# The first loads and steps of a fused attention and rational-MLP kernel, put in another order on one Trainium2 core

## The chip, the cores and the metric

The kernel runs on one NeuronCore of a Trainium2 chip. The metric is the device time of one execution in microseconds. The kernel before was timed three times: 251.33, 251.53 and 252.5, median 251.53.

## The reference

```python
def phi(x):
    a = np.einsum('rd,bhsd->bhsr', S1, x)
    b = np.einsum('rd,bhsd->bhsr', S2, x)
    return np.einsum('bhsi,bhsj->bhsij', a, b).reshape(*x.shape[:-1], r * r)
q_p, k_p = phi(q), phi(k)
kv = np.einsum('bhsf,bhsd->bhfd', k_p, v)
z = np.sum(k_p, axis=2)
attn = (q_p @ kv) / (q_p . z + 1e-6)
x = attn, heads side by side: (4352, 128)

h = x @ w_in
P = a[0] + a[1] * h + a[2] * h**2 + a[3] * h**3
Q = 1.0 + abs(b[0]) * abs(h) + abs(b[1]) * h**2
out = (P / (Q + 1e-06)) @ w_out
```

q, k and v are (4, 4, 1088, 32) in float32: 4 batches, 4 heads, 1088 tokens of 32 values. S1 and S2 are 8 x 32. w_in is 128 x 2048, w_out 2048 x 128. So there is a linear attention with quadratic sketch features, and behind it a two-layer network with a rational activation.

## The kernel before

**Stages.** Each batch goes through key steps, query steps and then the network. Key steps (class `Keys`): `kt` transposes a part of k in 32 x 32 blocks on DVE (L315), `ks` multiplies it with S1 and S2 on PE (L323), `kc` copies half of that from PSUM on ACT (L330), `kf` multiplies the halves on DVE to the features k_p (L335), and `kp` multiplies k_p with v on PE, the key products (L364). `kk` copies the result to kvz on ACT (L374). The first batch has k in four transposes and three parts, so that the work can begin before all of k is there: parts 0 and 1 hold two column blocks each, part 2 the other five.

**Queries.** Tokens go in blocks; the first batch has four. For each: `qt` transpose (DVE, L387), `qs` sketches (PE, L400), `qc` copy (ACT, L407 or L410), `qf` features (DVE, L416 or L419), `qp` products with kvz (PE, L428), `qd` the denominator plus 1e-6, `qi` its reciprocal, `qx` the quotient (DVE, L444, L449), `qb` transpose back (PE, L455) and `qk` copy to xT (ACT, L462). The fourth block and all later batches use class `Spread`, whose sketches (L473) go through DRAM (sk_d) and come back as `a_all` and `b_all` (L484 to L490).

**The network.** For each unit of up to 512 tokens, `h` multiplies xT with w_in on PE (L519), `e` casts the result to bf16 on ACT (L525), and DVE and ACT form the rational function (`u`, `ln`, `ex`, `rd`, `s`, `pd`, `m`, `v`, `x`); `G` multiplies with w_out on PE (L677) and `st` stores. `wo` scales the halves of w_out by constants that are computed from a and b.

**Order.** The program is written out by hand: the string `ORDER` lists all steps, each with an index, and every engine gets its instructions in that order. An engine works its list in order, so an instruction that waits holds up all behind it on that engine. Loads are steps too: `lk`, `lv`, `lq`, `lx` (w_in), `lw` (w_out); they are issued by SP. Eight semaphores serve all loads of SP and ACT in turn, so a load can have to wait until an earlier one with the same semaphore has landed.

**The first loads** stand ahead of `ORDER` (L196 to L214). SP issues S2, three quarters of k (240 KB, L201), 512 columns of the first q (256 KB, L206) and the four loads of v (L187). ACT issues S1, the first columns of each k block (256 KB, L199), the rest of k (48 KB, L203), a, b, and then loads its function table (L213). One load of v brings one column block m for all heads to 32 partitions; source and destination both begin with a dimension of 32:

```python
for m in range(NM):
    w = min(W, (NJ - m * NT) * D)
    nc.sync.dma_start(out=t[m * 32:(m + 1) * 32, :, 0:w], in_=vv[:, :, m * W:m * W + w])
```

**Idle products.** `tn` multiplies a tile of zeros on PE, 128 x 512 in bf16 (L225); `TURNS` says how many: 11 for `tn:0` and 2 for `tn:4`, all at the very start.

**Constants.** `ba` takes the absolute value of b on ACT (L818) and then runs a row of tiny steps on GpSimd (L759 to L772); `bi` takes a reciprocal on DVE (L775) and ends them. A second variant of the whole program (`General`) follows under a condition and isn't executed for these inputs.

Of the kernel before, what the change touches and what calls it, by code (L numbers as in the profile page):

```python
# [28 lines left out]
pd0:0 u0:0 kc0:1 kc1:1 kf0:1 m0:0 kt0:2 ln1:0 h0:1 e2:1 kt1:2 ex1:0 e0:1 v0:0 rd1:0 h1:1 ks1:2 qs:4 kf1:1 h3:1 qt:5  # L29
e1:1 h1:2 v1:0 u0:1 qf:3 qc:4 ln0:0 kc1:2 e3:1 ex0:0 kp1:1 qp:3 pd1:1 kf1:2 h3:2 ln0:1 s1:0 e1:2 rd0:0 qd:3 qi:3 G3:0  # L30
h0:2 ex0:1 e3:2 kk:1 e0:2 G0:0 x1:0 G5:0 qx:3 u1:1 qf:4 qs:5 qp:4 s0:0 u0:2 ln1:1 h2:2 lq:2 lk:3 qc:5 qd:4 qi:4 ex1:1
qt:7 qx:4 qb:3 qk:3 qb:4 lv:2 qk:4 x0:0 rd0:1 m1:1 ks0:2 qs:7 e2:2 u1:2 ln0:2 rd1:1 h2:3 v0:1 h0:3 e2:3 h1:3 v1:1
kc0:2 kf0:2 kt1:3 s1:1 ex0:2 qt:9 qf:5 e0:3 e1:3 kt0:3 ln1:2 G3:1 G2:0 h3:3 x1:1 h0:4 qc:7 e3:3 h3:4 ra0:2 st:0 qp:5
ex1:2 qd:5 qi:5 e0:4 ra1:2 kp1:2 s0:2 qx:5 G0:2 qs:6 u1:3 pd1:2 e3:4 qb:5 h1:4 qk:5 m0:2 G0:1 m1:2 h0:5 s1:2 qf:7
ln0:3 qc:6 e1:4 ln1:3 h2:4 x0:2 v1:2 G2:1 e0:5 ex1:3 qt:8 x1:2 pd1:3 h3:5 G1:2 kk:2 e2:4 ks0:3 ex0:3 qp:7 u1:4 e3:5
qs:8 ln0:4 rd0:3 rd1:3 h2:5 qd:7 e2:5 G3:2 qf:6 qc:8 s1:3 h1:5 G2:2 kc0:3 ln1:4 G5:1 kf0:3 qi:7 e1:5 lq:3 ex0:4 ex1:4
h1:6 G5:2 m1:3 h3:6 qx:7 u1:5 G3:3 ra0:4 qs:9 qp:6 x1:3 G0:3 rd1:4 G2:3 e1:6 ln0:5 st:2 pd1:4 lv:3 s1:4 h0:6 e3:6
ln1:5 qd:6 qi:6 qb:7 qf:8 G4:3 qx:6 qk:7 h2:6 m1:4 e0:6 qc:9 G0:4 ex1:5 qb:6 qk:6 qp:8 qt:10 ks1:3 h2:7 e2:6 G3:4
ex0:5 u1:6 x1:4 e2:7 h0:7 qd:8 ln1:6 G5:3 rd1:5 qi:8 h3:7 G1:4 G5:4 qt:12 G1:3 e0:7 G2:4 pd1:5 rd0:5 ex1:6 e3:7 h1:7
m1:5 kc1:3 ra1:6 qf:9 ln0:6 qx:8 e1:7 qp:9 qs:10 ex0:6 v0:5 qd:9 h1:8 s1:5 G4:4 u1:7 pd1:6 qc:10 h3:8 e1:8 st:4 qt:11  # L40
v1:5 rd0:6 qi:9 qb:8 G3:5 ln0:7 kf1:3 e3:8 ln1:7 h0:8 h2:8 x1:5 qk:8 qs:11 e0:8 ex1:7 kp1:3 s1:6 qx:9 G0:5 e2:8 G5:5
ex0:7 h2:9 kk:3 qf:10 h3:9 u1:8 qb:9 ra0:7 m0:6 G0:6 ra1:7 qs:12 m1:6 qc:11 x0:6 ln0:8 v1:6 e3:9 pd1:7 e2:9 qp:10 qk:9
qd:10 s1:7 G2:5 ln1:8 x1:6 G3:6 h0:9 qi:10 e0:9 h1:9 m1:7 ex0:8 qx:10 e1:9 pd1:8 v1:7 h1:10 u1:9 e1:10 rd0:8 ex1:8
rd1:8 G0:7 h0:10 G2:6 ln1:9 G3:7 e0:10 G1:6 ex1:9 qb:10 v0:7 h2:10 qk:10 e2:10 h3:10 s1:8 G5:6 qf:11 qp:11 ln0:9 h3:11
rd1:9 e3:10 h0:11 qd:11 ex0:9 m1:8 qi:11 e3:11 e0:11 u1:10 G3:8 G4:8 h2:11 x1:7 h1:11 x0:7 G2:7 ln1:10 qc:12 rd0:9
ln0:10 x1:8 e2:11 e1:11 G0:8 s1:9 ex1:10 ex0:10 G5:7 G1:8 h1:12 qx:11 qb:11 ra1:10 pd1:9 h0:12 qk:11 m1:9 u1:11 G0:9
x1:9 e1:12 G2:8 e0:12 h3:12 h2:12 rd0:10 qf:12 ln1:11 ln0:11 G5:9 G5:8 G1:9 s1:10 e2:12 G3:9 qp:12 ex0:11 pd1:10 e3:12
G0:10 ex1:11 m1:10 u1:12 rd0:11 h2:13 G3:10 ln1:12 ln0:12 e2:13 h3:13 qd:12 e3:13 G4:9 G2:9 rd1:11 h1:13 ex0:12 x1:10
h0:13 st:6 e1:13 s1:11 u1:13 ex1:12 pd1:11 m1:11 e0:13 G3:11 rd0:12 h2:14 ln1:13 h3:14 e2:14 G2:10 u0:13 ln0:13 G4:10
e3:14 qi:12 G1:11 x1:11 G1:10 rd1:12 qx:12 h1:14 ex1:13 st:8 s1:12 pd1:12 ex0:13 h0:14 e1:14 G0:11 qb:12 e0:14 ra0:13  # L50
rd1:13 G1:12 G5:10 G5:11 G4:11 qk:12 G3:12 h0:15 u1:14 ln0:14 m1:12 ln1:14 st:10 h1:15 x1:12 G0:12 G2:11 e0:15 h3:15
G4:12 ex1:14 e1:15 h2:15 s1:13 ex0:14 G3:13 pd1:13 m0:13 u0:15 G5:12 rd1:14 m1:13 e3:15 ln0:15 h1:16 e2:15 G4:13 G0:13
# [18 lines left out]
class General:  # L71
    FAST = False
    TURNS = (11, 0, 0, 0, 2, 0, 0, 0, 0)
# [49 lines left out]
def run(  # L123
# [26 lines left out]
    NM = 4  # L150
# [43 lines left out]
    for i, s_in in enumerate((S1, S2)):  # L194
        t = consts.tile([128, D], FP, name=f"s_raw{i}")
        (nc.scalar, nc.sync)[i].dma_start(out=t, in_=bass.AP(tensor=s_in.tensor, offset=s_in.offset,  # L196
                                                             ap=[[0, 16], [D, R], [1, D]]))
        s_raw.append(t)
# [75 lines left out]
    b_fit, c_fit, c_inv = (consts.tile([128, 2], FP, name=x) for x in ("b_fit", "c_fit", "c_inv"))  # L274
    a_k = consts.tile([128, 3], FP, name="a_k")
    special = consts.tile([128, 1], mybir.dt.int32, name="special")
    k_in_reg, k_sq_reg = (nc.scalar.alloc_register(x) if fast else None for x in ("k_in_reg", "k_sq_reg"))
    a1, a2, a3 = a_sb[:, 1:2], a_sb[:, 2:3], a_sb[:, 3:4]
# [299 lines left out]

    def on_act(i, h):
        return plan.P_ON_ACT[2 * i + (h > 0)]  # L580
# [68 lines left out]
    @skip()  # L649
    def d_v(i, h, hh):  # L650
        if horner(i, h):
            g = part_of(i, "g", h)
            nc.vector.tensor_scalar(out=g, in0=g, scalar1=a1, scalar2=None, op0=AX.add)

    @skip(plan.WIDE_X, horner)
    def d_g(i, h, hh):
        g = part_of(i, "g", h)
        nc.vector.tensor_mul(out=g, in0=g, in1=part_of(i, "s" if horner(i, first(h)) else "p", h))  # L658

    def terms(i):  # L660
# [96 lines left out]
    def fitting():  # L757
        g = nc.gpsimd
        g.tensor_mul(out=sq, in0=ab0, in1=ab0)  # L759
# [5 lines left out]
        by(fit, b4, AX.is_ge, sq, AX.mult, fit)  # L765
        by(lim, fit, AX.mult, -1.0, AX.add, 1.0)
# [3 lines left out]
        g.tensor_copy(out=special, in_=lim)  # L770
        by(c_fit[:, 1:2], b4, AX.mult, 1.0 + 1e-6, AX.subtract, sq)
        g.tensor_copy(out=c_fit[:, 0:1], in_=b_fit[:, 0:1])  # L772

    def factors():
# [3 lines left out]
        nc.gpsimd.tensor_copy(out=a_k[:, 2:3], in_=k_out)  # L778
        by(k_in, b4, AX.mult, 0.5, AX.mult, c_inv[:, 0:1])
        by(k_sq, sq, AX.mult, c_inv[:, 1:2])  # L780

    def registers():
        nc.scalar.reg_load(k_in_reg, k_in[0:1, :].bitcast(mybir.dt.int32))
        nc.scalar.reg_load(k_sq_reg, k_sq[0:1, :].bitcast(mybir.dt.int32))
        if any(plan.P_ON_ACT):
            nc.scalar.reg_load(a3_reg, a_sb[0:1, 3:4].bitcast(mybir.dt.int32))
# [9 lines left out]
    does = {"e": evac, "h": hidden, "u": d_abs, "w": d_w, "y": d_y, "ln": a_square if fast else a_ln, "ex": a_root if fast else a_exp, "ra": a_inv, "rd": d_inv, "pa": a_p, "pd": d_p,  # L796
# [7 lines left out]
    for step in plan.ORDER:  # L804
# [63 lines left out]
```

## Time and profile before

| | |
|---|---|
| median of three runs | 251.53 us |
| the profiled execution | 251.9 us, of which its span 250.0 |
| busy PE, DVE, ACT, GpSimd | 240.5, 233.0, 227.9, 7.5 us |
| first product of the network (L519) | starts at 18.05 us in the chain |
| moved by DMA | 19.60 MB |

All times inside the kernel count from the start of the span. In a list of work the columns are start, duration, engine, line, operation, tiles, count, and in brackets the idle time of the engine in front of it with what ended that time. PE is the matmul array, PEld its weight load, which runs beside it, SPq and ACTq are the DMA issues of SP and ACT. A float32 product appears as two passes, so 36 instructions give 72 entries. In the chain of waits each piece is the one that the next had to wait for.

### The profile page before, as it was taken

How to read it: one execution, taken by the hardware profiler on the slowest of the kernel's cores; microseconds unless marked ns; L12 is line 12 of the kernel's file. 1: busy time of each engine (PE TensorE's matmuls, PEld its weight loads, DVE VectorE, ACT ScalarE, POOL GpSimd, SP SyncE). 2: the span in 40 equal slices, each digit the busy share in tenths (PEclk: the TensorE clock that was granted, in tenths of full speed). 3: DMA queues.
4: the chain of work that ended last, by engine and by line, in shares of the span. 5: the costliest groups of instructions: out<-in, count | busy, mean ns of one | idle time of the engine just before them, and what ended most of it. 6: DMA issues, size and time to landing. Idle time of an engine off the chain costs nothing.

```text
span 250.0 us, 4083 instructions
## 1 busy us (share of the span) xinstructions
PE 240.5 (96%) x1585; PEld 133.8 (54%) x1585; DVE 233.0 (93%) x233; ACT 227.9 (91%) x217; POOL 7.5 (3%) x43
## 2 busy tenths in 40 slices
PE   7889999999999999999999999999999999999990
PEld 2668546645645455445555344444544467666770
DVE  3776999899999999999999999999999999999990
ACT  2267999999999999999999999999999999999980
POOL 4340000000000000000000000000000000000000
PEclk9999999999999999999999999999999999999999
DMA  5995348464413176210512200030020211020032
GB/s 155 257 387 89 99 121 188 134 156 78 144 27 100 28 202 138 69 45 16 148 22 77 67 3 0 16 102 3 0 42 0 40 25 22 0 37 8 0 49 42
DMA packets 30534, 19.60 MB, mean 78 GB/s; under 512 B 20400, under 2 KB 26672, under 8 KB 30512
## 3 DMA queue, kind: packets, MB, share of 16 engines
q1 hardware_dynamic: 28864, 18.92, 30.4%
q10 hardware_dynamic: 1648, 0.40, 0.9%
q8 instruction: 13, 0.21, 0.4%
q14 instruction: 9, 0.07, 0.1%
HBM read 16.16 MB, written 3.15 MB: 77 GB/s over the span
## 4 chain that ended last, share of the span: by engine, by line
PE 77%; DVE 13%; DMA 3%; issue 3%; SPq 0%; DVEq 0%
PE h_ps L519 42%; PE att_ps L677 23%; PE att_ps L428 4%; DVE g L658 4%; PE att_ps L364 4%; DVE g L647 3%; DVE s L643 2%; DMA k_sb<-in_k_dram 2%; PE att_ps L455 2%; DMA v_sb<-in_v_dram 2%; PE att_ps L473 2%; PE att_ps L323 1%; DVE p L600 1%; DVE r L630 1%; DVE out_sb L686 1%
## 5 line engine op out<-in xcount | busy, mean ns | idle before, releaser
L519 PE MATMUL h_ps<-xT,w_in_sb 128*128 128x512 f32 (+1 forms) x320 | 125.8, 532 | 0.0
L519 PEld LDWEIGHTS h_ps<-xT,w_in_sb 128*128 128x128 f32 x320 | 59.3, 190 | 44.4 <-issue 34.0
L525 ACT CAST hh<-h_ps 128x1024 bf16<-128x1024 f32 x68 | 72.2, 1086 | 2.1 <-PE h_ps L519 1.9
L613 ACT ACTIVATE ln<-u 128x2048 f32<-128x2048 bf16 (+1 forms) x35 | 67.2, 1950 | 0.0
L677 PEld LDWEIGHTS <-w_out 128*128 128x128 bf16 x432 | 41.8, 98 | 46.0 <-issue 16.5
L618 ACT ACTIVATE r<-ln 128x2048 bf16<-128x2048 f32 x22 | 44.0, 2002 | 0.0
L643 DVE TENSOR_TENSOR s<-hh,r 128x4096 bf16<-128x4096 bf16 (+2 forms) x21 | 39.2, 1872 | 0.0
L677 PE MATMUL att_ps<-r,w_out 128*128 128x512 bf16 (+1 forms) x160 | 34.8, 347 | 0.1
L677 PE MATMUL att_ps<-g,w_out 128*128 128x512 bf16 (+1 forms) x160 | 34.4, 347 | 0.0
L647 DVE TENSOR_TENSOR g<-hh,s 128x4096 bf16<-128x4096 bf16 (+2 forms) x16 | 27.8, 1744 | 0.3 <-PE att_ps L677 0.3
L658 DVE TENSOR_TENSOR g<-g,p 128x4096 bf16<-128x4096 bf16 (+2 forms) x15 | 27.7, 1849 | 0.0
L630 DVE TENSOR_TENSOR r<-r 128x2048 bf16<-128x2048 bf16 x22 | 26.5, 1217 | 0.0
L677 PE MATMUL att_ps<-s,w_out 128*128 128x512 bf16 (+1 forms) x112 | 24.5, 349 | 0.4 <-DVE s L643 0.4
L618 ACT ACTIVATE ln<-ln 128x2048 f32<-128x2048 f32 (+1 forms) x13 | 24.4, 1895 | 0.0
L624 ACT ACTIVATE r<-ln 128x2048 bf16<-128x2048 f32 (+1 forms) x13 | 23.7, 1868 | 0.0
L600 DVE TENSOR_SCALAR p<-hh,a_sb 128x4096 bf16<-128x4096 bf16 (+1 forms) x17 | 21.6, 1273 | 0.6 <-ACT hh L525 0.6
L548 DVE TENSOR_SCALAR u<-hh 128x2048 uint16<-128x2048 uint16 (+2 forms) x24 | 21.7, 905 | 0.4 <-ACT hh L525 0.4
L647 DVE TENSOR_TENSOR g<-hh,p 128x2048 bf16<-128x2048 bf16 (+1 forms) x7 | 11.6, 1663 | 0.0
L658 DVE TENSOR_TENSOR g<-g,s 128x2048 bf16<-128x2048 bf16 (+1 forms) x8 | 11.6, 1463 | 0.0
L428 PEld LDWEIGHTS att_ps<-kvz,q_pT 128*64 128x64 f32 x288 | 9.8, 137 | 3.3 <-issue 1.7
L428 PE MATMUL att_ps<-kvz,q_pT 128*64 128x66 f32 x288 | 11.1, 224 | 0.0
L364 PE MATMUL att_ps<-v_sb,k_p 128*64 128x64 f32 (+1 forms) x288 | 9.2, 222 | 1.0 <-DMA v_sb<-in_v_dram 1.0
(79 smaller groups left out, 146.6 us busy)
## 6 DMA issues: line engine op xcount, KB each, us to landing
a_all<-sk_d SPq DMA_DIRECT2D x6, 384.0 KB
b_all<-sk_d SPq DMA_DIRECT2D x12, 192.0 KB
v_sb<-in_v_dram SPq DMA_DIRECT2D x12, 144.0 KB
k_sb<-in_k_dram SPq DMA_DIRECT2D x3, 544.0 KB
q_sb<-in_q_dram SPq DMA_DIRECT2D x3, 544.0 KB
a_all<-sk_d SPq DMA_DIRECT2D x4, 320.0 KB
b_all<-sk_d SPq DMA_DIRECT2D x8, 160.0 KB
w_out_sb_f<-in_moe_w_out_dram SPq DMA_DIRECT2D x2, 512.0 KB
```

The costliest lines, as they stand in the source:

```text
L428: nc.tensor.matmul(self.nd[g * 64:(g + 1) * 64, o:o + 2 * KW], lhsT=self.q_p[:, c, x + g * 64:x + (g + 1) * 64], rhs=kvz[self.b % 2][:, c, ...
L519: nc.tensor.matmul(t[:, x * tl:(x + 1) * tl], lhsT=w_in_sb[:, f * 128:(f + 1) * 128], rhs=xT[:, x_at(t0):x_at(t0) + tl], start=True, stop= ...
L525: nc.scalar.copy(out=live[i]["hh"][:, part * PW:(part + 1) * PW], in_=live[i]["h", part])
L600: nc.vector.tensor_scalar(out=part_of(i, "p", h), in0=hh, scalar1=a3, scalar2=a2, op0=AX.mult, op1=AX.add)
L613: nc.scalar.activation(out=t, in_=live[i]["u"][:, span(h)], func=ACT.Square, scale=k_in_reg, bias=1.0)
L618: nc.scalar.activation(out=t if r_on_act(i, h) else part_of(i, "r", h), in_=t, func=ACT.Abs_reciprocal_sqrt, scale=k_sq_reg, bias=1.0)
L624: nc.scalar.activation(out=part_of(i, "r", h), in_=live[i]["ln", h], func=ACT.Square)
L630: nc.vector.tensor_mul(out=t, in0=t, in1=t)
L643: nc.vector.tensor_mul(out=part_of(i, "s", h), in0=hh, in1=part_of(i, "r", h))
L647: nc.vector.tensor_mul(out=part_of(i, "g", h), in0=hh, in1=part_of(i, "p" if horner(i, first(h)) else "s", h))
L658: nc.vector.tensor_mul(out=g, in0=g, in1=part_of(i, "s" if horner(i, first(h)) else "p", h))
L677: nc.tensor.matmul(outs[t0][:, :tl], lhsT=w_sb[y][:, f0 + x, :], rhs=part_of(i, key, h)[:, c:c + tl], start=done[0] == 0, stop=done[0] == ...
```

## The change

S1 is issued by SP too, so that ACT's first load is k. v is loaded directly behind SP's part of k and ahead of q, in one load per head over all 128 partitions; the source is walked column block by column block, so that its outermost dimension is 4. (The last block of each row group also brings 64 columns that nobody uses.) ACT loads its table ahead of b and a, and b comes before a. `tn:0` has 8 products instead of 11, and the 2 of `tn:4` stand behind the key sketches. In `ORDER`, the steps ahead of `ex0:1` stand otherwise; from there on the two orders are the same. The squared form of the polynomial, which the diff also brings (`SQ`, `VDMA`, `WIDE_V`), is off: these lists are empty. What is left of it is two more small copies on GpSimd and a reciprocal of four columns instead of two.

```diff
-    TURNS = (11, 0, 0, 0, 2, 0, 0, 0, 0)
+    SQ = ()
+    VDMA = ()
+    WIDE_V = ()
+    TURNS = (8, 0, 0, 0, 2, 0, 0, 0, 0)
     ORDER = """
-tn:4 tn:0 lw:1 lq:0 kt0:0 lw:0 kt1:0 lx:1 kt2:0 lx:0 ks1:0 kt3:0 ks0:0 lk:1 qt:0 ks2:0 kc0:0 kc1:0 kf0:0 kf1:0 qs:0
-kc2:0 qt:1 kf2:0 qc:0 kp0:0 ba:0 kp1:0 qf:0 kp2:0 qt:3 qs:1 kk:0 bi:0 qt:2 lq:1 lv:1 qc:1 qf:1 qp:0 qd:0 qs:2 qi:0
-qx:0 qb:0 wo:3 qc:2 qk:0 qf:2 wo:0 qp:1 qs:3 qp:2 qd:1 wo:5 wo:1 h2:0 qd:2 wo:4 e2:0 qi:1 h3:0 qx:1 qi:2 h0:0 wo:2
-qx:2 qb:1 rg:0 kt0:1 e3:0 e0:0 qb:2 pd1:0 qk:2 h1:0 kt1:1 u1:0 m1:0 lk:2 qk:1 e1:0 qc:3 ks0:1 ks1:1 qt:6 qt:4 h2:1
...
+lx:0 kt1:0 tn:0 kt0:0 kt3:0 lq:0 kt2:0 ks0:0 ks1:0 ks2:0 tn:4 kc1:0 kf1:0 kc0:0 kf0:0 kc2:0 lx:1 kp0:0 qt:0 ba:0 kp1:0
+qs:0 kf2:0 qt:1 qc:0 qf:0 kp2:0 qt:2 kk:0 qs:1 qp:0 bi:0 qs:2 qc:1 lw:1 qd:0 qf:1 qi:0 qx:0 lk:1 qc:2 qb:0 qt:3 qk:0
+lw:0 qp:1 wo:5 qf:2 wo:1 lq:1 wo:3 qd:1 kt1:1 qs:3 kt0:1 lk:2 qc:3 qi:1 qp:2 h2:0 qd:2 e2:0 rg:0 qx:1 h3:0 qi:2 h0:0
+qx:2 wo:4 qb:2 wo:2 qb:1 ks0:1 e3:0 pd1:0 wo:0 ks1:1 e0:0 qk:1 u1:0 kc0:1 m1:0 qk:2 qt:4 h1:0 kt0:2 h2:1 ln1:0 e1:0
...
     for i, s_in in enumerate((S1, S2)):
         t = consts.tile([128, D], FP, name=f"s_raw{i}")
-        (nc.scalar, nc.sync)[i].dma_start(out=t, in_=bass.AP(tensor=s_in.tensor, offset=s_in.offset,
+        nc.sync.dma_start(out=t, in_=bass.AP(tensor=s_in.tensor, offset=s_in.offset,
...
     nc.scalar.dma_start(out=k0[:, km + 4 * D:S], in_=k0_src[:, km + 4 * D:S])
+    for h in range(H):
+        nc.sync.dma_start(out=v_bufs[0][:, h, 0:W],
+                          in_=bass.AP(tensor=v.tensor, offset=v.offset + h * S * D, ap=[[W, NM], [S * D // 32, 32], [1, W]]))
     q0 = io.tile([128, S], FP, name="q_sb", bufs=1)
     q0_src = q[0].rearrange("h (g j) d -> (h g) (j d)", g=32)
     nc.sync.dma_start(out=q0[:, 0:512], in_=q0_src[:, 0:512])
+    nc.scalar.preload_act_table_set("abs_reciprocal_sqrt_and_small" if fast else "natural_log_exp_and_others")
     a_sb = consts.tile([128, 4], FP, name="a_sb")
     b_sb = consts.tile([128, 2], FP, name="b_sb")
+    nc.scalar.dma_start(out=b_sb, in_=bass.AP(tensor=moe_b.tensor, offset=moe_b.offset,
+                                              ap=[[0, 128]] + list(moe_b.ap)))
     nc.scalar.dma_start(out=a_sb, in_=bass.AP(tensor=moe_a.tensor, offset=moe_a.offset,
                                               ap=[[0, 128]] + list(moe_a.ap)))
-    nc.scalar.dma_start(out=b_sb, in_=bass.AP(tensor=moe_b.tensor, offset=moe_b.offset,
-                                              ap=[[0, 128]] + list(moe_b.ap)))
-    nc.scalar.preload_act_table_set("abs_reciprocal_sqrt_and_small" if fast else "natural_log_exp_and_others")
-    load_v(0)
```

The source of `a_all` (L487) is walked as 16 x 8 rows and that of each of the two `b_all` (L490) as 8 x 8 rows, in both kernels.

More of the change, by code (lines that the diff above doesn't have):

```diff
@@ L33 @@
[L33 to L37, printed above, removed]
@@ L72 @@
     FAST = False
+    SQ = ()
+    VDMA = ()
+    WIDE_V = ()
     TURNS = (11, 0, 0, 0, 2, 0, 0, 0, 0)
@@ L273, in run @@
     sq, lim, fit, b4, k_in, k_sq, k_out = (consts.tile([128, 1], FP, name=x) for x in ("sq", "lim", "fit", "b4", "k_in", "k_sq", "k_out"))
-    b_fit, c_fit, c_inv = (consts.tile([128, 2], FP, name=x) for x in ("b_fit", "c_fit", "c_inv"))
+    b_fit, a_lim, a_fit = (consts.tile([128, 2], FP, name=x) for x in ("b_fit", "a_lim", "a_fit"))
+    c_fit, c_inv, a_abs = (consts.tile([128, 4], FP, name=x) for x in ("c_fit", "c_inv", "a_abs"))
+    k_p, gam, delta = (consts.tile([128, 1], FP, name=x) for x in ("k_p", "gam", "delta"))
     a_k = consts.tile([128, 3], FP, name="a_k")
     special = consts.tile([128, 1], mybir.dt.int32, name="special")
-    k_in_reg, k_sq_reg = (nc.scalar.alloc_register(x) if fast else None for x in ("k_in_reg", "k_sq_reg"))
-    a1, a2, a3 = a_sb[:, 1:2], a_sb[:, 2:3], a_sb[:, 3:4]
+    k_in_reg, k_sq_reg, k_p_reg = (nc.scalar.alloc_register(x) if fast else None for x in ("k_in_reg", "k_sq_reg", "k_p_reg"))
+    a_n = consts.tile([128, 4], FP, name="a_n")
+    a_part = a_n if fast and plan.SQ else a_sb
+    a1, a2, a3 = (a_part[:, x:x + 1] for x in (1, 2, 3))
+    add_h, add_sq = a1, delta
+    kinds = [any(2 * i + h in plan.VDMA and 2 * i + h in x for i in range(17) for h in range(2)) if fast else False for x in (plan.HORNER, plan.SQ)]
+    RW = 1024 if all(kinds) else 2048
+    rows = [big.tile([128, RW], BF, name=f"row{x}") if kinds[x] else None for x in range(2)]
     a3_reg = nc.scalar.alloc_register("a3_reg" if fast else "a3_reg_g")
@@ L577, in horner, with squared @@
         return 2 * i + (h > 0) in plan.HORNER
+    def squared(i, h):
+        return 2 * i + (h > 0) in plan.SQ
     def on_act(i, h):
@@ L595, in first, with a_psq @@
         return 0 if h == "both" else h
+    @skip()
+    def a_psq(i, h, hh):
+        assert squared(i, h)
+        nc.scalar.activation(out=part_of(i, "g", h), in_=hh, func=ACT.Square, scale=k_p_reg, bias=1.0)
     @skip(plan.WIDE_P, on_act)
     def d_p(i, h, hh):
+        assert not squared(i, first(h))
         if not on_act(i, first(h)):
@@ L665, in terms @@
             cuts[1:] = [(per // 2, 3 * per // 4), (3 * per // 4, per)]
-        return [[(x, y, key) for x in range(*c)] if y != 1 or not horner(i, n) else []
+        return [[(x, y, key) for x in range(*c)] if y != 1 or not (horner(i, n) or squared(i, n)) else []
                 for n, c in enumerate(cuts) for y, key in enumerate(("r", "s", "g"))]
@@ L758, in fitting @@
         g = nc.gpsimd
+        aa1, aa2, aa3 = (a_abs[:, x:x + 1] for x in (1, 2, 3))
         g.tensor_mul(out=sq, in0=ab0, in1=ab0)
@@ L765, in fitting @@
         by(fit, b4, AX.is_ge, sq, AX.mult, fit)
+        if plan.SQ:
+            by(a_lim[:, 0:1], aa3, AX.mult, 2.0 ** -10)
+            by(a_lim[:, 1:2], aa1, AX.mult, aa3, AX.mult, 8.0)
+            g.tensor_mul(out=gam, in0=aa2, in1=aa2)
+            by(fit, aa3, AX.is_ge, 2.0 ** -20, AX.mult, fit)
+            by(fit, aa3, AX.is_le, 2.0 ** 20, AX.mult, fit)
+            by(fit, aa2, AX.is_ge, a_lim[:, 0:1], AX.mult, fit)
+            by(fit, a_lim[:, 1:2], AX.is_ge, gam, AX.mult, fit)
         by(lim, fit, AX.mult, -1.0, AX.add, 1.0)
@@ L769, in fitting @@
         g.tensor_mul(out=sq, in0=b_fit[:, 0:1], in1=b_fit[:, 0:1])
-        g.tensor_copy(out=special, in_=lim)
+        if plan.SQ:
+            by(a_fit, a_sb[:, 2:4], AX.mult, fit, AX.add, lim)
+        else:
+            g.tensor_copy(out=a_fit, in_=b_fit)
         by(c_fit[:, 1:2], b4, AX.mult, 1.0 + 1e-6, AX.subtract, sq)
         g.tensor_copy(out=c_fit[:, 0:1], in_=b_fit[:, 0:1])
+        g.tensor_copy(out=c_fit[:, 2:4], in_=a_fit)
+        g.tensor_copy(out=special, in_=lim)
     def factors():
@@ L777, in factors @@
         by(a_k[:, 0:2], a_sb[:, 0:2], AX.mult, k_out)
-        nc.gpsimd.tensor_copy(out=a_k[:, 2:3], in_=k_out)
+        if not plan.SQ:
+            nc.gpsimd.tensor_copy(out=a_k[:, 2:3], in_=k_out)
         by(k_in, b4, AX.mult, 0.5, AX.mult, c_inv[:, 0:1])
         by(k_sq, sq, AX.mult, c_inv[:, 1:2])
-    def registers():
[L783 to L786, printed above, removed]
+        if plan.SQ:
+            by(gam, a_fit[:, 0:1], AX.mult, a_fit[:, 0:1])
+            by(gam, gam, AX.mult, 0.25, AX.mult, c_inv[:, 3:4])
+            by(a_k[:, 2:3], k_out, AX.mult, gam)
+            by(k_p, a_fit[:, 1:2], AX.mult, 2.0, AX.mult, c_inv[:, 2:3])
+            by(gam, k_p, AX.mult, 2.0, AX.mult, c_inv[:, 2:3])
+            by(a_n, a_sb, AX.mult, gam)
+            by(delta, a1, AX.add, -1.0)
+    def registers():
+        loads = [(k_in_reg, k_in), (k_sq_reg, k_sq)]
+        loads += [(k_p_reg, k_p)] * bool(plan.SQ) + [(a3_reg, a3)] * any(plan.P_ON_ACT)
+        for reg, x in loads:
+            nc.scalar.reg_load(reg, x[0:1, :].bitcast(mybir.dt.int32))
+        for row, x in zip(rows, (add_h, add_sq)):
+            if row is not None:
+                n = RW // 512
+                nc.scalar.activation(out=row.rearrange("p (c x) -> p c x", c=n), in_=idle[:, None, :].to_broadcast([128, n, 512]),
+                                     func=ACT.Identity, bias=x, scale=1.0)
     value = []
@@ L819, in run @@
             if fast:
+                if plan.SQ:
+                    nc.scalar.activation(out=a_abs, in_=a_sb, func=ACT.Abs)
                 fitting()
```

67 lines of the change are left out of this document (41 added, 26 removed).

## The prediction

> **What bounds the kernel now.** I read first how full the engines are in each stretch of the span, then the chain of work that ended last. The first fence is the page; the second is the table by stretches, whose columns are length, busy time of PE, PEld, DVE, ACT and POOL with their instruction counts, granted clock, busy share of the 16 DMA engines, GB/s.
>
> ```profile
> span 250.0 us, 4083 instructions
> ```
>
> ```profile
> 0.00:18.05 18.05, 14.92 (x200) 9.37 (x200) 10.88 (x27) 5.74 (x16) 7.46 (x43) 1.00 0.87 263
> 18.05:45.00 26.95, 26.95 (x237) 17.77 (x237) 24.27 (x34) 24.89 (x31) 0.00 (x0) 1.00 0.55 133
> ...
> 204.00:240.00 36.00, 35.56 (x196) 24.71 (x195) 36.00 (x29) 36.00 (x28) 0.00 (x0) 1.00 0.14 21
> ```
>
> From 18.05 on PE has no idle time worth the name, and at the end DVE and ACT have none either. PE cannot catch up, so whatever moves the first product of the dense part (h2:0 at L519, 18.05 us) moves the end by about as much. The question is only what the opening does. Its chain (start, length, what):
>
> ```profile
> 1.59 4.42 DMA k_sb<-in_k_dram
> 6.01 0.02 issue
> 6.03 3.98 DMA v_sb<-in_v_dram
> 10.01 0.25 issue
> 10.26 2.32 PE att_ps L364 x72
> 12.58 1.06 PE h_ps L400 x8
> 13.64 0.64 PE att_ps L428 x16
> 14.29 0.00 issue
> 14.29 0.44 DVE qT L387
> ...
> 16.22 0.41 PE att_ps L455 x2
> 16.63 0.62 PE att_ps L428 x16
> 17.25 0.34 PE att_ps L473 x4
> 17.59 0.47 PE att_ps L428 x16
> 18.05 5.38 PE h_ps L519 x24
> ```
>
> The opening waits for transfers: k is there at 6.01, v at 10.01, and only then come the 72 passes of the key products (L364), done at 12.58. From there 5.47 us lead to h2:0. Each of the 36 instructions stands twice in the trace.
>
> **The change: v.** v becomes four loads of 128 partitions x 1152 B, 590 KB in all. The load's source now begins with a dimension of 4 (the column blocks), where it began with 32. The trace has two loads of that kind that differ only there: a_all (source begins with 16) and the pair b_all (begins with 8). Their issues, and the share of DMA engines while they were in flight:
>
> ```profile
> 29.86 0.54 SPq L487 DMA_DIRECT2D a_all<-sk_d  x1
> 30.45 1.33 SPq L490 DMA_DIRECT2D b_all<-sk_d  x2
> ```
>
> ```profile
> 32.00:32.50 0.50, 0.50 (x15) 0.43 (x16) 0.50 (x2) 0.50 (x2) 0.00 (x0) 1.00 0.95 333
> ...
> 33.00:33.50 0.50, 0.50 (x5) 0.30 (x2) 0.50 (x2) 0.50 (x2) 0.00 (x0) 1.00 0.48 133
> 33.50:34.00 0.50, 0.50 (x2) 0.19 (x1) 0.50 (x1) 0.50 (x3) 0.00 (x0) 1.00 0.58 164
> ```
>
> With a_all at work nearly all 16 engines are busy; with the two b_all alone, about half are. Two loads on different halves would have filled all 16, so both sat on the same eight, one after the other. A leading 4 should then leave v four engines, again the same four for all heads. Price: a quarter of 333 GB/s is 83, and 590 KB take 7.1 us. Bounds: half of 133 GB/s is 67, so 8.8 us; a quarter of 408 GB/s (below) is 102, so 5.8 us. I take 7.1, from the row with full engines.
>
> The Trainium skill, page "DMA: Bandwidth & Descriptors", section "Why a DMA increments its semaphore by 16 and not by 1", says it outright: a transfer uses the largest number up to 16 that divides the slowest dimension of both its sides, and always the lowest-numbered engines. For 4 and 128 that is four engines; the rows above agree for 8, and no run so far shows 4.
>
> **k, and q behind v.** ACT's queue loses S1, so its part of k is issued 0.73 us earlier; SP's part goes out behind two S loads instead of one, some half a microsecond later.
>
> ```profile
> 0.82 0.68 ACTq L196 DMA_DIRECT2D s_raw<-in_S_dram  x1
> 1.55 0.60 ACTq L199 DMA_DIRECT2D k_sb<-in_k_dram  x1
> ```
>
> The same bytes begin sooner: I take k whole at 5.5 (bounds 5.3 and 6.0). On the four engines v is then through at 5.5 + 7.1 = 12.6, against 10.01 before. The first piece of q (256 KB), which landed ahead of v, now stands behind it on every engine that v uses: at some 350 GB/s, 0.7 us more, 13.3.
>
> ```profile
> 16.00:18.00 2.00, 1.78 (x39) 1.57 (x39) 2.00 (x6) 1.93 (x5) 0.00 (x0) 1.00 1.02 408
> ```
>
> Behind that queue stand w_in, the rest of q, w_out and the next k, some 2.9 MB; at 333 to 408 GB/s they pass in 7 to 9 us, by 22.3 at the latest. The second half of w_in is wanted at about 21.5 and is third of six; the last, half of w_out, is wanted at about 24. They cost nothing while v takes under 8 us; v at 8.8 makes itself late first.
>
> **The new order on PE and DVE.** Durations:
>
> ```profile
> 1.26 5.69 PE L225 MATMUL att_ps<-idle 128*128 128x512 bf16 x13 [1.26 <-DVE idle L220]
> ...
> 7.19 0.45 DVE L387 STREAM_TRANSPOSE qT<-q_sb 128x256 f32<-128x256 f32 x1 [0.32 <-DMA q_sb<-in_q_dram]
> ...
> 9.42 1.45 DVE L335 TENSOR_TENSOR k_p<-h_ps,b_sk 128x1280 f32<-128x1280 f32 x1
> ...
> 12.65 0.51 DVE L387 STREAM_TRANSPOSE qT<-q_sb 128x320 f32<-128x320 f32 x1 [1.17 <-DMA q_sb<-in_q_dram]
> ...
> 16.65 0.75 DVE L419 TENSOR_TENSOR q_pT<-att_ps,a_all 128x256 f32<-128x256 f32 x2
> ```
>
> DVE now has the transpose of the first q block (qt:0) ahead of the last key features (kf2), and waits there for q: 13.3 + 0.45 + 1.45 = 15.2. PE does the key products of parts 0 and 1 (32 of 72 passes, 1.0 us) from 12.6 on, then the q sketches (1.06, from 13.75), both inside that wait; then the last 40 passes, 2.32 x 40/72 = 1.3: done at 16.5, against 12.58. That is **+3.9**. From there to h2:0 the old way took 5.47 us. In the new order the third q transpose (qt:2, 0.44) is done in front of these steps, while PE is at the key products, so 5.0 remain: qt:3 and its successor on DVE (0.51 and 0.75) just fit beside PE's 0.41 + 0.62 + 0.34. h2:0 starts at 21.5 instead of 18.05: **+3.45**.
>
> Work on other engines: b and a are issued behind the table load, b's absolute value comes before the first q copy, and the GpSimd steps that follow it get two more small copies. They end in this reciprocal:
>
> ```profile
> 14.21 0.17 DVE L775 RECIPROCAL c_inv<-c_fit 128x2 f32<-128x2 f32 x1 [1.05 <-POOL c_fit L772]
> ```
>
> DVE waited 1.05 us for GpSimd there. The next DVE step now (the first `den`) follows products of about 18, so even at its old time the reciprocal lies 3.6 us ahead; without that cover two copies more would cost some 0.4. v of the next batch is issued later on SP, behind the spread transfers of the fourth q block; its products stood at 36 us and will stand later, and the queue is empty by then. The changed places of w_out and of the next k transposes only fill DVE's and ACT's gaps between 18 and 45 us.
>
> **Three idle products fewer, and PE's rate.** The clock column reads 1.00 from the start, but the 13 idle products took 5.69 us, 0.43 us apart. In the dense part:
>
> ```profile
> 191.56 3.45 PE att_ps L677 x16
> ```
>
> Products of the same width are 0.216 us apart, so PE ran all 13 at half rate, over 5.5 us. Eight take 3.4 us, end at 4.7, and k's transposes leave a gap before the sketches. Then PE stands from about 8.5 to 12.6. Whether it has reached full rate by then the trace cannot show. If so, the cost is nothing. If not, a column takes 0.43/512 us and a pass of 64 columns 0.053: parts 0 and 1 take 1.7 instead of 1.0, the sketches (8 passes of 256) run from 14.3 to 16.0, and the 40 passes follow at full rate (done at 17.3, +0.8) or half (done at 18.1, +1.6). Bounds 0 and 1.6; by the row of 13 slow products I count the first two as slow and, after 3.4 us of them on top of all that went before, the 40 passes as fast: +0.8.
>
> By the Trainium skill ("TensorE: Matmul & The Clock Gate", Part 1) a window of about 3.4 us of sustained work raises the clock, and the windows run freely; eight products would then just do if a window fell on them, and the sum would be 0.8 less. The row speaks against counting on it: 5.5 us of work went by at half rate here.
>
> **Sum.** 3.45 + 0.8 = **+4.25 us**. The profiled execution took 251.9 us (its span is 250.0), so 256.15 for its like; it lies 0.37 above the median of 251.53, and against that median the forecast is **255.8 us**.
>
> **Rivals.**
> *v uses all engines (the other side: faster).* For it: k, q and w_in, whose sources begin with 128, fill them (the 408 GB/s row). Against: the b_all rows. Then v takes 1.7 us at 350 GB/s, stands at 7.2 and q at 7.9; the last key products end at 7.9 + 0.45 + 1.45 + 1.3 = 11.1, h2:0 starts at 16.1: -1.95, **249.6 us**. With PE at half rate it queues from about 8.4 on, when the two idle products behind the key sketches end: 1.7 + 1.7 and 1.3 to 2.1 make 13.1 to 13.9, so 251.6 to 252.4. It decides at the point where q lands by 9.4 (12.58 less the same three terms): v's 590 KB in under 3.2 us, or at least eight engines.
> *Full rate, four engines:* +3.45, **255.0 us**. It is the forecast without its last term.
> *The delay is taken up again.* DVE ends the chain, and has 26.95 - 24.27 = 2.7 us idle between 18.05 and 45; if PE had slack, only 1.55 of the 4.25 would reach the end: **253.1 us**. Against it: PE's 26.95 of 26.95, which are products back to back.
>
> **How the numbers follow.** Four engines 0.76 (at half rate for the key products 0.42, the forecast; full rate 0.34). Delay taken up 0.05. All engines 0.19, of which 0.10 with the full gain and 0.09 with the half rate eating it. A measurement here tells about 0.5% (1.26 us) from no change, so faster 0.10, same 0.09, slower 0.81. Range: four engines give 3.45 - 1.3 to 3.45 + 1.7 + 1.6, so 253.7 to 258.3; taking in the case of delay taken up and the half-rate end of the fast rival, **251.6 to 258.3**.
>
> **What would show it.** While v is in flight, a DMA share near 0.25 and some 80 GB/s between 6 and 12.5 us; DVE's first qT waiting for q until about 13; k_p of the last part after it; the 72 passes ending past 16; the first L519 at 21 to 23. Half rate shows as passes of L364 0.05 us apart where they are 0.03 now. The forecast is wrong if the share is near 1 with v landed by 8, or if L519 starts late and the span does not follow.

## The result, and the profile after

The changed kernel takes **260.41 us** (median of six runs, 259.76 to 261.71); the kernel before, run on the same chip, 251.57. The ratio is 1.0352, with an interval of 1.0322 to 1.0382: 8.84 us slower. The forecast was 255.8 with a range up to 258.3. The sign and the main mechanism were right; the 4.25 us that were forecast are about half of what came.

The profiled execution of the changed kernel took 261.71 us, the longest of the six, and its span is 9.8 us longer than that of before. Its page, and the table by stretches (columns as above: length, busy time of PE, PEld, DVE, ACT and POOL, granted clock, DMA share, GB/s), cut at the start of the dense part as it was for before:

```profile
span 259.8 us, 4063 instructions
```

```profile
0.00:26.29 26.29, 17.92 (x197) 12.20 (x197) 10.10 (x27) 5.68 (x16) 7.71 (x45) 0.81 0.65 173
26.29:53.24 26.95, 26.95 (x237) 17.87 (x238) 25.44 (x35) 24.98 (x31) 0.00 (x0) 1.00 0.48 143
...
212.24:248.24 36.00, 35.41 (x194) 24.71 (x196) 36.00 (x30) 36.00 (x28) 0.00 (x0) 1.00 0.14 22
```

The opening is 26.29 us long where it was 18.05. Behind it PE is as full as before. The chain of waits through the opening:

```profile
1.58 4.30 DMA s_raw<-in_S_dram
5.89 0.02 issue
5.91 9.35 DMA v_sb<-in_v_dram
15.25 0.04 issue
15.30 1.76 PE att_ps L380 x26
17.05 2.01 PE h_ps L416 x8
19.07 2.24 PE att_ps L380 x40
21.30 1.06 PE h_ps L416 x8
...
26.29 0.84 PE h_ps L535 x3
```

Three things are to be seen. v is whole at 15.25, not at 10.01 (the key products are L380 here). The pieces behind it are slow: 40 passes of L380 took 2.24 us, which is 0.056 a pass, while all 72 took 2.32 before (0.032). And the chain now begins with S2, the second load of SP, which took 4.30 us to land, and whose semaphore the fourth load of v waits for (its issue waited 1.2 us for it).

The end is also later by itself. The last pieces of the two chains, after first and before second:

```profile
252.24 0.45 DVE out_sb L722
```

```profile
244.14 0.45 DVE out_sb L686
```

From h2:0 to the end of this piece it is 226.40 us after and 226.54 before: the dense part gives nothing back and costs nothing. From there to the end of the span it is 7.1 us after and 5.4 before. So the 9.8 us of the two profiled executions are 8.24 in the opening, -0.14 in the dense part and 1.7 behind the last copy. The forecast had no term for the last one.

### The profile page after: what moved, and what is told of

The parts are those of the page before. It is cut to its first block, busy times and chain, and to the rows that moved or that the text cites. A ratio compares the mean times of both kernels' runs of the same rounds, so it can differ in the third digit from the quotient of the medians.

```text
span 259.8 us, 4063 instructions
## 1 busy us (share of the span) xinstructions
PE 242.2 (93%) x1566; PEld 136.8 (53%) x1582; DVE 232.7 (90%) x233; ACT 227.8 (88%) x217; POOL 7.7 (3%) x45
## 4 chain that ended last, share of the span: by engine, by line
PE 31%; ACT 27%; DVE 24%; issue 8%; DMA 6%; SPq 1%; DVEq 0%; ACTq 0%
PE h_ps L535 15%; PE att_ps L713 11%; ACT ln L638 9%; ACT hh L541 8%; DVE g L694 5%; DVE g L672 4%; DMA v_sb<-in_v_dram 4%; ACT r L643 3%; DVE s L668 3%; DVE r L655 3%; ACT ln L643 2%; DVE p L625 2%; DMA s_raw<-in_S_dram 2%; ACT r L649 2%; PE att_ps L380 2%
## 5 line engine op out<-in xcount | busy, mean ns | idle before, releaser
L713 PE MATMUL att_ps<-r,w_out 128*128 128x512 bf16 (+1 forms) x152 | 33.6, 346 | 0.7 <-issue 0.3
L713 PE MATMUL att_ps<-g,w_out 128*128 128x512 bf16 (+1 forms) x155 | 33.4, 346 | 0.3 <-issue 0.2
L643 ACT ACTIVATE ln<-ln 128x2048 f32<-128x2048 f32 (+1 forms) x13 | 24.5, 1903 | 0.0
L380 PE MATMUL att_ps<-v_sb,k_p 128*64 128x64 f32 (+1 forms) x288 | 12.1, 245 | 4.1 <-DMA v_sb<-in_v_dram 4.0
L380 PEld LDWEIGHTS att_ps<-v_sb,k_p 128*64 128x64 f32 (+1 forms) x288 | 11.1, 158 | 6.8 <-issue 3.6
L403 DVE STREAM_TRANSPOSE qT<-q_sb 128x384 f32<-128x384 f32 (+2 forms) x13 | 6.5, 502 | 6.2 <-DMA q_sb<-in_q_dram 6.2
```

Source lines behind the costliest of these rows:

```text
L380: nc.tensor.matmul(out.rearrange("p (n d) -> p n d", d=D), lhsT=self.k_p[part][:sl, t - self.PARTS[part][0], 2 * c + a].rearrange("p i j - ...
L643: nc.scalar.activation(out=t if r_on_act(i, h) else part_of(i, "r", h), in_=t, func=ACT.Abs_reciprocal_sqrt, scale=k_sq_reg, bias=1.0)
L713: nc.tensor.matmul(outs[t0][:, :tl], lhsT=w_sb[y][:, f0 + x, :], rhs=part_of(i, key, h)[:, c:c + tl], start=done[0] == 0, stop=done[0] == ...
```

## The experiments

Fourteen kernels were run, each against the kernel before on the same chip; the intervals are those of the ratio to it. The theory to begin with (theory 1) is that of the prediction, with the sizes from the trace: v's four engines carry most of the loss, the other loads and the clock the rest.

### v's shape, undone and alone

The changed kernel with v loaded by block as before:

```diff
-    for h in range(H):
-        nc.sync.dma_start(out=v_bufs[0][:, h, 0:W], ...)
+    load_v(0)
```

> The changed kernel, but v is again loaded column block by column block for all heads (source begins with 32), in the new place behind k; all else of the change stays. Theory 1 (the four engines of the new v loads are the cause): v lands near 9.5 us instead of 15.25 and the first q near 10.3 instead of 15.75, the last key products end at 13.3 to 14 instead of 21.3, and the time is 252 to 253 us. Theory 2 (the two S loads on one queue are the main cause, since S2 landed at 5.9 us and k and v start behind it): the time stays above 257. Theory 3 (eight idle products leave PE at half rate): above 257 as well.

Measured: 254.48 us, ratio 1.0114 (1.007 to 1.0158). Undoing the shape gives back 5.9 us, but 2.7 stay, more than the theory left (252 to 253). Its chain:

```profile
2.20 4.91 DMA k_sb<-in_k_dram
...
10.17 1.50 PE att_ps L378 x32
11.67 1.06 PE h_ps L414 x8
12.73 1.31 PE att_ps L378 x40
...
19.02 3.67 PE h_ps L533 x16
```

v has left the chain, and k (landed at 7.11) stands in it. The dense part starts only 1.0 us later than before, and the time from the last product to the end is 6.5 us instead of 5.9. Together they account for the 1.4 us by which the span of the profiled execution is longer than that of before. But that execution was the fastest of the four (253.3), and what the median has beyond it no trace shows.

The kernel before with the four loads by head in the old place, behind q, and nothing else:

> The kernel before with one thing changed: its first v is loaded per head over 128 partitions (source begins with 4), in its old place behind the first q. Theory 1: share of DMA engines near 0.25 while v is alone, v lands at 14 to 15.5 us, and as w_out, the rest of q and w_in stand behind it on the same four engines, the first network product starts at about 24 instead of 18; the time is 256 to 259 us. Theories 2 and 3 expect no more than 2 us over the kernel before, 253.5 us.

Measured: 258.02, ratio 1.0242 (1.0192 to 1.0292), as theory 1 said; v was whole at 15.51 and h2:0 came at 24.5. Alone, the shape costs 6.3 us, and there is no S1 and no new order to blame.

### Four engines, or one queue?

Heads 1 and 3 of v issued by ACT:

```diff
-        nc.sync.dma_start(out=v_bufs[0][:, h, 0:W],
+        (nc.sync, nc.scalar)[h % 2].dma_start(out=v_bufs[0][:, h, 0:W],
```

> The changed kernel with heads 1 and 3 of v issued by ACT, heads 0 and 2 by SP. Theory 1 (the four loads share the same four DMA engines, whatever the queue): v is whole no earlier than 14.3 (8.5 us of packets on four engines, from 6 on), the time is 259.0 to 261.5. Rival (one queue passes its loads one after the other, so v was slow because all four stood on SP's): two loads run beside two, v is whole by 11, the last key products end by 17, the time is 255 to 257.

Measured: 257.8, ratio 1.023 (1.0202 to 1.0257). Both numbers of theory 1 missed, and the rival's too. The chain:

```profile
3.81 9.30 DMA v_sb<-in_v_dram
13.11 0.14 issue
13.24 1.76 PE att_ps L380 x28
```

v is whole at 13.11, 2.1 us sooner than in the changed kernel, because the loads are issued sooner (the last of the four at 3.81 instead of 5.91). The load itself takes as long: 9.30 us from that last issue, against 9.35. Two queues do not halve it, so the queue is not what puts the four in series. The packet records of the traces say the same: v's packets of 1152 B keep about 4.2 engines busy between 7 and 14 us in the changed kernel, and about 4.3 between 7 and 11 in this one, where two queues feed them. Not all of the 2.6 us by which this kernel is faster than the changed one is v's: SP issues 149 transfers here instead of 151, and from the last product to the end it is 6.3 us instead of 7.6 ("One more transfer on SP", below).

The changed kernel with the loads of w_in, the rest of q, w_out and the next k moved behind the first q copy on ACT, so that v flies almost alone:

> The changed kernel with the loads of w_in, the rest of q, w_out and the next k issued by ACT behind its first q copy, so that nothing but k and the first piece of q is in flight beside v. Only the landing of v is read; the time gets worse, since these loads are late. Theory 1 (v's packets slow down because the other loads share the memory or the engines): packets stay near 0.051 us, v is whole 6.4 to 7.2 us after it begins, at 12.4 to 13.4. Rival (four engines pass 590 KB no faster than 8.5 us): v is whole at 14.6 to 15.4.

One execution took 264.24 us, since the moved loads are late; v was whole at 12.74, as theory 1 said. The table for a stretch in which v flies, in this kernel and then in the changed one (the last two columns are the DMA share and GB/s):

```profile
9.00:11.50 2.50, 0.76 (x6) 0.52 (x6) 0.00 (x0) 0.00 (x0) 1.92 (x8) 1.00 0.27 97
```

```profile
9.00:11.50 2.50, 1.94 (x10) 0.70 (x6) 0.53 (x1) 0.40 (x2) 1.47 (x6) 0.63 1.05 266
```

Alone, v keeps 0.27 of the sixteen engines busy, about four, at 97 GB/s. In company the other twelve are at work on w_in and the rest of q, and the share is full although v is no faster. In the chain it shows as 7.28 us instead of 9.35:

```profile
5.46 7.28 DMA v_sb<-in_v_dram
```

So the company costs v some 2 us: the prediction's 7.1 was between the 6.6 us that v needs alone (from 6.18, where SP's part of k landed, to 12.74) and the 8.5 that it took in the changed kernel (6.72 to 15.25). The packet records show where: a packet of v takes 51 ns from 7 us to the end when v is nearly alone, and in the changed kernel 51 between 7 and 9 us and 75 to 83 between 9 and 14, when w_in and the loads behind it are in flight too.

### S1 on ACT again

```diff
-        nc.sync.dma_start(out=t, in_=bass.AP(tensor=s_in.tensor, ...
+        (nc.scalar, nc.sync)[i].dma_start(out=t, in_=bass.AP(tensor=s_in.tensor, ...
```

In the changed kernel:

> The changed kernel with S1 issued by ACT again, ahead of its part of k. Theory 1: S2 lands near 4 instead of 5.9 and SP's part of k near 6.0 instead of 6.7, so v starts and ends 0.7 to 1.2 us earlier, and 259.2 to 259.8 us come out. Theory 2: 254 us or less. Theory 3: no change, 260.4.

Measured: 258.88, ratio 1.0274 (1.0227 to 1.0321), 1.5 below the changed kernel, where theory 1 gave it 0.6 to 1.2. The same edit with v by block:

> The changed kernel with v by block again and S1 on ACT again; against the run with the new order and eight idle products only three things are left: q behind v, b ahead of a, and the table ahead of both. Theory 1 (q's place costs, because DVE's first q transpose stands ahead of the last key features): q lands at 9.6 to 10.0, k_p of the last part ends at 11.5 to 11.9, the key products at 13.0 to 13.8, h2:0 starts at 18.3 to 18.9, the time is 252.0 to 253.2 and above the run with the new order and eight by 0.5 to 1.2. Rival (q's place is hidden, and it was S1's move that left 2.7 us with v by block): equal to the run with the new order and eight within 0.3.

Measured: 253.08, ratio 1.0055 (1.0036 to 1.0074), 1.4 below the run with v by block and S1 on SP. That q's place costs anything fell here: this kernel has q behind v and is 1.4 us faster than the one with the new order and eight products (254.44, next section), which has q in front. The rival, that the two are equal within 0.3, fell with it.

### The order and the idle products

The kernel before with the new `ORDER` and eight idle products, then with eleven, and at last with none; the loads are the old ones:

```diff
-    TURNS = (11, 0, 0, 0, 2, 0, 0, 0, 0)
+    TURNS = (8, 0, 0, 0, 2, 0, 0, 0, 0)
```

> The kernel before with the new opening order and the eight idle products alone; all its loads (S1 on ACT, v by block behind q, a and b ahead of the table) stay as they were. Theory 1 (the loads make nearly all of the loss, order and idle products cost little): k is there at 6.0 and v at 10.0 again, DVE's first q transpose no longer waits for q (7.2), the last key features end at 11.1 and the key products at 12.6 to 13.2 (some passes may be at half rate); h2:0 starts at 17.6 to 18.5, the time is 251.2 to 252.4. Rival (the new order or the lost idle products carry the 2.7 us that were left when v went back to its old shape): 253.3 to 254.5, with h2:0 past 19.

> As the run with the new order and eight idle products, but with 11 of them as before. If the granted clock with eight falls back to half between 7.5 and 11 (as it did with v by block) and stays full with eleven, this one is faster by what the slow passes cost: 0.2 to 1.0 us. If the clock keeps full either way, both agree within 0.3 us. Theory 1: 251.0 to 252.0; rival (the order itself costs): 253 or more.

> The run with the new order and the old loads, with no idle products in the opening (those behind the key sketches stay at 2). Theory (in most executions the eight raised nothing, or the clock fell again, and the key products ran at half rate): the granted clock first becomes full past 8 us, the time is 254.2 to 255.2, like most executions of the run with eight (254.4). Rival (eight do their work and the 1.9 us between eight and eleven had another cause): 255.5 or more, since even that work is gone now.

Measured: eight 254.44, ratio 1.0105 (1.0084 to 1.0125); eleven 252.5, 1.0036 (1.0012 to 1.006); none 253.7, 1.0077 (1.0052 to 1.0103), nine of its executions between 252.09 and 254.71 and one at 255.9. Eight came out in the range of the rival, eleven between the two ranges. Three products fewer cost 1.9 us, twice what was expected at most, and eight are no better than none. In the run with none the granted clock was first full at 9.88, past 8 as expected, but its time missed its range below and the rival's by far.

The changed kernel with 16 instead of 2 products behind the key sketches, and with 34:

> The changed kernel with 16 instead of 2 idle products behind the key sketches, so that PE is at work until v lands. Theory 1 with PE's clock as a term of the sum: the clock stays full, the 26 waiting passes take 0.8 us instead of 1.76, the sketches 1.1 instead of 2.1, and the last key products end near 19 instead of 21.3: 257.9 to 258.5 us. Theory 3 (clock is the main cause): 254 or less. If the clock costs nothing: 260.4.

> The changed kernel with 34 products instead of 2 behind the key sketches, enough to keep PE at work until v is there. Theory (the price of the half rate is what its slow passes add on the chain: 26 passes 1.76 instead of 0.9, 40 passes 2.31 instead of 1.4, the sketches behind them 1.06 instead of 0.6 to 1.0): the granted clock stays full from 5 on, the last key products end at 18.9 to 19.5, h2:0 starts at 23.5 to 24.2, the time is 257.9 to 258.9. Rival (the half rate costs only the 0.8 us that the prediction took): 259.3 to 260.0.

Measured: 259.13, ratio 1.0278 (1.0236 to 1.032), and 260.85, ratio 1.037 (1.0355 to 1.0385). The 16 gain 1.3 us, less than expected. They were done at 11.5, and PE waited for v again: between 11.91 and 15.33 it had 1.25 us of work. The granted clock, full from 5.09 on, fell to half at 15.33. So the first 26 passes took 1.03 us instead of 1.76, but the sketches (2.08) and most of the other 40 passes (1.84 in all) ran at half rate again; the clock was full from 18.75 on. The 34 did not do what they were made for. PE's list:

```profile
9.35 9.42 PE L233 MATMUL att_ps<-idle 128*128 128x512 bf16 x34
18.70 1.15 PE L380 MATMUL att_ps<-v_sb,k_p 128*64 128x64 f32 x32
...
20.85 1.39 PE L380 MATMUL att_ps<-v_sb,k_p 128*64 128x64 f32 x40
```

34 products at full rate (0.216 each) are 7.3 us; they took 9.42, because in this execution the eight at the start had not raised the clock, and the granted clock became full only at 13.25. PE was still at them when v had long landed. So the price of the half rate can't be read from this run's time, which missed both ranges above. But its key products ran at full rate, as its chain shows:

```profile
18.77 1.08 PE att_ps L380 x32
19.85 1.06 PE h_ps L416 x8
20.92 1.32 PE att_ps L380 x40
```

These three pieces take 3.46 us, where they took 6.0 in the changed kernel (15.30 to 21.30). The run also shows that whether eight raise the clock is not settled by the kernel.

The last run with v by block, S1 on ACT and the new order, with eleven instead of eight:

> The run with q behind v (S1 on ACT, v by block, b and a on ACT, the new order) with eleven idle products instead of eight. SP issues 150 transfers, so the end should be the short one (5.8 to 6.3 us behind the last product). Theory (eight products raise the granted clock only when one of its free windows happens to fall on them, eleven nearly always): PE is at full rate from 5 to 7 us on, the last key products end at 12.4 to 12.9, h2:0 starts at 17.4 to 17.9, the time is 251.2 to 252.0, 1 to 2 us under the run with eight (253.1). Rival (the number of idle products means nothing once v stands ahead of q): 252.8 to 253.4.

Measured: **251.66**, against 251.68 for before; ratio 1.0011 (1.0 to 1.0022). All that is left of the change in this kernel, the new order, v ahead of q, b ahead of a and the table ahead of both, makes no difference that can be told. Its chain:

```profile
5.26 3.98 DMA v_sb<-in_v_dram
...
9.63 1.15 PE att_ps L378 x32
10.79 1.06 PE h_ps L414 x8
11.85 1.32 PE att_ps L378 x40
...
18.14 5.38 PE h_ps L533 x24
```

The key products end at 13.17 (12.58 before), because the q sketches stand between their two parts; but these are then done, and h2:0 starts at 18.14 (18.05). Both are later than expected, though the time lies in its range.

The same loads with b and a issued by SP behind q, so that v's third and fourth load need not wait for k's semaphores:

> The run with q behind v (S1 on ACT, v by block) with two edits: eleven idle products again, and b and a issued by SP behind q, so that the third and fourth v load no longer wait for the semaphores of k. If v's place ahead of q gains what that run's trace showed against the run with q ahead (key products begun 1 us earlier, h2:0 0.5 us earlier, although PE was at half rate until 10.4), then v is whole by 8.0 to 8.5, q's first piece by 9.0, the last key products end at 11.9 to 12.6, h2:0 starts at 16.8 to 17.6, and the time is 250.6 to 251.6, at or below the kernel before (251.74). Rival (that gain was an accident of the profiled execution): 252.3 to 253.1, as the runs with the new order and eleven, or with q behind v.

Measured: 253.35, ratio 1.0068 (1.0049 to 1.0087). The opening came close to what was expected (the first L533 starts at 17.76, the last key products end at 12.86), and yet the time is 1.7 us above the run before it and above both ranges. Here the end was long again: 7.1 us from the last product to the end of the span, against 5.65 in the run before.

### One more transfer on SP

In every profile up to here, SP with 151 or 152 transfers went with ten loads of 8 KB on the queue that the page calls q14, and 145 to 150 transfers with nine; the tenth comes last of all, behind the last product. From the last product to the end it is 6.48 to 7.61 us in the profiles with ten and 5.65 to 6.27 in those with nine. The test leaves the opening alone: in the kernel before, a late load (q of the last batch) is split in two, so that SP issues 151 instead of 150.

```diff
-        nc.sync.dma_start(out=t, in_=q[b].rearrange("h (g j) d -> (h g) (j d)", g=32))
+        src = q[b].rearrange("h (g j) d -> (h g) (j d)", g=32)
+        for x, y in ((0, 512), (512, S)) if b == 3 else ((0, S),):
+            nc.sync.dma_start(out=t[:, x:y], in_=src[:, x:y])
```

> The kernel before with one late load on SP split in two (q of the last batch, wanted past 100 us), so that SP issues 151 transfers instead of 150, as the changed kernel does; the opening is untouched. Theory (in all profiles so far SP's program with one or two transfers more goes with ten instead of nine loads of 8 KB on the instruction queue, the tenth behind the last product, and with 6.5 to 7.6 us from the last product to the end instead of 5.8 to 6.3; the longer program is the cause): h2:0 stays at 18.0, ten such loads, the end 0.6 to 1.7 us later, the time 252.1 to 253.2. Rival (the longer end is chance, or comes from something else in the changed kernel): nine such loads, 251.3 to 251.8.

Measured: 252.97, ratio 1.0054 (1.0039 to 1.0068): **1.29 us** for one transfer more by the medians, and h2:0 was even a little earlier (17.80). In the profiled execution (252.36, the second fastest of six) the end is 0.6 us longer. The pages' line of that queue, of this kernel, then of the kernel before:

```profile
q14 instruction: 10, 0.08, 0.1%
```

```profile
q14 instruction: 9, 0.07, 0.1%
```

The changed kernel has ten as well. The 151st transfer in it is S1. That the tenth load is a further piece of SP's own program is argued from the count of SP's transfers in all sixteen profiles, not seen.

### The sum by single edits

| kernel | us | step |
|---|---|---|
| changed | 260.41 | |
| v by block again | 254.48 | -5.9 |
| S1 on ACT again too | 253.08 | -1.4 |
| eleven idle products too | 251.66 | -1.4 |
| before | 251.54 to 251.77 | 0 |

The rows come from different chips, on which the kernel before differs by 0.23 us at most. A step also depends on what else is in the kernel: eleven products instead of eight gained 1.4 us here and 1.9 with the old loads.

No run beats the kernel before by anything that can be told.

## Why the prediction was right in kind and short in size

**What bounds the kernel** was right. The dense part passed the delay on unchanged (226.40 against 226.54 us), and the rival in which the delay is taken up again is out. What failed is the sum for the opening, by which h2:0 should have come at 22.3 and came at 26.29, and a term for the end that it did not have.

**v on four engines** was right. The share of 0.27 while v flies almost alone shows it, and the run on two queues shows that the engines and not the queue are shared. By the rule on page "DMA: Bandwidth & Descriptors" of the Trainium skill, section "Why a DMA increments its semaphore by 16 and not by 1", a leading 4 against 128 partitions gives four engines, and the 0.27 agrees. The prediction's sign for it was badly chosen, though: a share near 0.25 between 6 and 12.5 was never there, since the loads behind v went ahead on the other twelve engines.

**"I take k whole at 5.5"** failed: SP's part (240 of k's 544 KB, not three quarters as said above) landed at 6.72, outside the bounds too. That was 1.2 us. S2 now stands second on SP, beside ACT's k, and landed at 5.89. Every transpose of k stands on DVE behind that of S2, which waits for it, and the issue of the fourth v load waits for S2 as well. The prediction counted SP's issue times and no landing of S2.

```profile
5.91 0.21 DVE L258 STREAM_TRANSPOSE sT<-s_raw 128x32 f32<-128x32 f32 x1 [1.71 <-DMA s_raw<-in_S_dram]
...
6.27 1.48 DVE L331 STREAM_TRANSPOSE kT<-k_sb 128x256 f32<-128x256 f32 x4
```

**"590 KB take 7.1 us"** was mis-sized: 8.5, within its bounds of 5.8 to 8.8. In the trace the difference is the other loads in flight: 6.6 without them.

**"+0.8" for PE's rate** was mis-sized, and outside the bounds of 0 to 1.6. The granted clock, in stretches cut where it changed:

```profile
4.01:7.42 3.41, 0.82 (x12) 0.34 (x12) 1.70 (x8) 0.00 (x0) 1.00 (x4) 1.00 0.41 107
7.42:10.83 3.41, 3.32 (x39) 2.14 (x34) 1.62 (x3) 0.72 (x4) 0.99 (x6) 0.50 0.95 266
10.83:14.25 3.42, 0.50 (x4) 0.25 (x3) 0.00 (x0) 0.00 (x0) 2.67 (x12) 1.00 1.01 242
14.25:21.08 6.83, 5.78 (x73) 4.85 (x74) 3.27 (x6) 0.58 (x1) 0.15 (x1) 0.50 0.92 264
21.08:26.29 5.21, 4.75 (x77) 3.59 (x75) 3.22 (x10) 3.09 (x10) 1.06 (x5) 1.00 0.20 57
```

The eight products did raise the clock, at 4.01. In the 3.41 us before, PE had been at work for 2.75. It then had 0.82 us of work in 3.41, and the next stretch was at half; that one was full of work, and the next was at full, in which PE waited for v; and so the key products got half. (The 6.83 are two stretches; in the first of them PE was at work for 2.36 us, which did not raise the clock yet.) In this trace each stretch has the clock that the work of the one before it earned. What the slow passes cost follows from DVE's two steps that PE needs there:

```profile
15.78 0.45 DVE L403 STREAM_TRANSPOSE qT<-q_sb 128x256 f32<-128x256 f32 x1 [6.24 <-DMA q_sb<-in_q_dram]
16.15 1.45 DVE L351 TENSOR_TENSOR k_p<-h_ps,b_sk 128x1280 f32<-128x1280 f32 x1
```

At full rate (40 passes 1.32, as in the run with v by block, eleven products and S1 on ACT) 26 passes take 0.86 and end at 16.16, the sketches run from 16.23 to 17.29, the last features are done at 17.60, and the 40 passes behind them would have ended at 18.96 (0.04 between the two engines). They ended at 21.30: 2.3 us. The three pieces at full rate in the run with 34 products (3.46 us instead of 6.0) fit this. I had taken the first slow products as the warm-up of the rest; the wait for v, which the same sum contained, undoes any warm-up. Page "TensorE: Matmul & The Clock Gate" of the Trainium skill, Part 1, has windows of about 3.4 us that run freely; the stretches here are 3.41 us or twice that, so the trace agrees.

**The new order** was right: 4.99 us from the last key products to h2:0, 5.0 forecast. **q behind v** was costed at 0.7 us and took 0.5 (15.25 to 15.75). **a and b** and **the later loads**, costed at nothing, cost nothing that can be told: the 4.99 us hold for the loads in the changed kernel, and the last kernel of the table has a and b in their new places.

**The end** was no step of the prediction at all. S1 on SP was weighed by its place in the opening, and not as one more instruction of SP's program. By the single edits it made 1.3 to 1.4 us of the 8.84.

In the profiled execution the opening's 8.24 us instead of 4.25 are thus about 1.2 for k, 1.4 for v and 1.5 for the rate, less 0.2 by which q followed v more closely than assumed; and 1.7 came at the end.

What stays open: S1 on ACT again gained 1.4 to 1.5 us by the medians, and the one transfer less on SP explains 1.3 of them, so in a median execution the late S2 can have cost little; in the profiled ones the opening was 1.4 us shorter with S1 on ACT (h2:0 at 24.80 instead of 26.21). The changed kernel's opening differs between executions by more than a microsecond (its twin with 16 products behind the sketches had S2 at 5.23 and h2:0 at 24.37), so the 1.2 us for k, and the split of the rest between the transfer and the clock, hold for the profiled execution only. Why S2 lands so late behind S1 on one queue was not tried by itself.

## What to carry to other kernels

Before a load is reshaped, look at the outermost dimension of its source: a 4 there made it a quarter as wide here, and loads of the same shape queued up on the same engines, whatever queue issued them. A kernel like this one, bound by PE from the first product of its dense part on, pays for a late transfer twice, since the clock falls while PE waits (half rate behind a stretch with 0.50 us of work in 3.42), and work that keeps the clock up must last until the data is there. And a transfer moved to another engine moves its instruction with it: compare the instruction loads at the end of the span before and after.

## What the runs showed that was not expected

- One more transfer on SP, the 151st, cost this kernel 1.29 us by the medians; with it came a tenth load of 8 KB on the instruction queue, behind the last product.
- Two 16 KB loads with 128 B pieces in a row on SP's queue, beside a 256 KB load on ACT's, landed at 3.96 and 5.89 (the second between 5.19 and 6.03 in the six profiles with both on SP); on two queues ahead of it, at 2.98 and 3.28.
- Eight idle products raised the granted clock by 5.1 us in five profiles with eight (4.01, 4.22, 4.96, 4.98, 5.09), and in four it stayed low until 9.35, 10.37, 13.25 and 19.59. Eleven raised it in all six profiles, between 4.92 and 6.79.
